# Raw expert weights loaded through the Activation queue during the attention stage of an attention + mixture-of-experts + MLP kernel

## The chip, the cores and the metric

The kernel runs on one core of a Trainium2 chip. The metric is the device time of one execution in microseconds. Before the change it is 692.5 us, the median of 3 runs (692.36 to 692.69).

## What is computed

Three layers follow each other. The first is causal attention with a decay (the running sum of log f) on 2 batches, 8 heads, 576 positions, 64 values a head. The second is a dense mixture of 4 experts with ReLU, weighted by normalised domain probabilities, and the third an MLP with x * sigmoid(1.702 x).

```python
def _attn_ref(q, k, v, f):
    scores = scale * np.matmul(q, k.transpose(0, 1, 3, 2))
    cum = np.cumsum(np.log(np.clip(f, 0.0001, 1.0)), axis=-1)
    scores = np.where(causal, -1e9, scores + cum[..., :, None] - cum[..., None, :])
    attn = softmax(scores)
    return np.matmul(attn, v)

def _moe_ref(x, domain_probs, w1, w2):           # x: 1152 x 512, E = 4, F = 1024
    p = domain_probs / (domain_probs.sum(-1, keepdims=True) + 1e-09)
    for e in range(E):
        out += p[:, e:e + 1] * (np.maximum(x @ w1[e], 0.0) @ w2[e])

def _moe2_ref(x, w_in, w_out):                   # F = 2048
    h = x @ w_in
    return (h * (1.0 / (1.0 + np.exp(-1.702 * h)))) @ w_out
```

## The kernel before

Products are made of rounded parts: each operand is split into a high part (rounded to float32r) and a low part (what is left), and three products of the parts are summed. A weight tile of 128 x 512 is split in two steps, by `split_w` (line 213): ScalarE (ACT) writes the high part `whi` (`round_act`, line 60), and later `rest` lets VectorE (DVE) write the low part `wlo` (line 230). Raw weights come two tiles at a time into a buffer `wst` of 512 KB (`load_owed`, line 188), of which there are four. A buffer is free once DVE has made the low parts of both its tiles.

The program runs over steps. The list `seq` holds units of work of the mixture (layer 1 or 2 of a visit of an expert half to a chunk of tokens), each unit a few steps. In the first 200 us the same loop also pulls the attention forward (`pull`), a pair of heads at a time: scores on TensorE (PE, line 587), the row maximum on DVE (617), the exponential on ACT (633), the normalisation by GpSimd (POOL, 643), transposes on PE (661), copies `ph` by ACT (line 60), the product with v on PE (691), and the split of its result into `xh` and `xl`. PE works on layer 1 (line 866) and layer 2 (1016) of the experts in between. Everything after `begin_late` (the joint products, line 904, and the MLP) has no attention in it.

The loads of the heads (`kq`, `qr`, `cb`, `cbs`, `vd`: keys, queries, the running sums spread over partitions, values) and those of the raw weights are all issued by SyncE (SP) through `load` (line 66), in one order. `cb` and `cbs` must wait until DVE has read the buffer that they overwrite, in its maximum of an earlier unit.

When a pair of weight tiles has been split, `rest` puts `load_pair` into `pair_due`, and it is called by the `rest` of the next tile that is split:

```python
        def rest():
            while pair_due:
                pair_due.pop()()
            (nc.gpsimd if v_ == 0 and kind == 'a' and g < 4 else nc.vector).tensor_sub(lf, raw, f(hf))
            if g % 2:
                ...
                pair_due.append(load_pair)
```

The order of each engine's instructions isn't the order of the code: the framework sets it by a scheduler that follows its own estimate of times, except where the code pins it (`in_turn`, `pin_turn`).

Of the kernel before, what the change touches and what calls it, by code (L numbers as in the profile page):

```python
# [39 lines left out]
def attn_moe_mlp(ctx: ExitStack, tc: tile.TileContext, qk0, qk1, qk2, v0, vp, fg, dp, wa_moe, wb_moe, wa_mlp, wb_mlp, out):  # L40
# [6 lines left out]
    nc = tc.nc  # L47
# [16 lines left out]
    def load(out, in_):  # L64

        ins = nc.sync.dma_start(out=out, in_=in_)
        if start[0]:
            tc.keep_in_program_order(ins)
# [8 lines left out]
    late = {}  # L77
# [16 lines left out]
    def scratch(i, o):  # L94
        return h_raw[i][:, o:o + 4 * WN]

    def tiles(c):

        t0, n = span[c]
        return range(t0 // 128, (t0 + (2 * n if c == EXP[0] else n)) // 128)  # L100
# [90 lines left out]
    def load_owed():  # L191

        while w_owed[0] and w_loaded[0] < len(w_pairs):
            kind, v_, g = w_pairs[w_loaded[0]]
            b = visits[v_][0]
            if b < NMOE:
                src = (wa_moe if kind == "a" else wb_moe)[b, g:g + 2]
            else:
                i = m_order.index((kind, v_, g))
                if m_made[0] < i + 2:  # L200
                    return
                src = wm[i:i + 2]
            w_owed[0] -= 1
            w_loaded[0] += 1
            t = wst_p.tile([128, 2, 512], F32, tag="wst", name="wst")
            load(t, src.rearrange("g p c -> p g c"))
            raw_w[kind, v_, g] = t[:, 0, :]
            raw_w[kind, v_, g + 1] = t[:, 1, :]

    lo_due, pair_due, lo_of = [], [], []  # L210

    def split_w(kind, v_, g):
        while (kind, v_, g) not in raw_w:
            next(cv_gen[0])
            load_owed()
        raw = raw_w.pop((kind, v_, g))
        p = wa_p if kind == "a" else late["wb"] if late and v_ % 2 else wb_p
        hi = p.tile([128, 4, 128], F32R, tag="hi", name="whi")
        lo = p.tile([128, 4, 128], F32R, tag="lo", name="wlo")
        hf = hi.rearrange("p a c -> p (a c)")  # L220
        lf = lo.rearrange("p a c -> p (a c)")
        round_act(hf, raw)
        (wa if kind == "a" else wb)[v_, g] = (hi, lo)
        if kind == "a" and v_ in joint:
            joint_raw[g] = raw
# [6 lines that stand above are left out]
                if kind == "a" and v_ in joint and v_ not in placed:  # L232
                    sum_weights(v_, g // 2)
                pair_due.append(load_pair)

        lo_due.append(rest)
        lo_of.append((kind, v_, g))
# [87 lines left out]
    def split_rest():  # L325
        lo_of.clear()
        while lo_due:
            lo_due.pop(0)()
# [82 lines left out]
    def begin_late():  # L411
        att_scope.close()
        start[0] = False
        late["ps"] = pool("ps_l", 5, PSUM)
        late["st"] = pool("mst", 2)
        late["wf"] = pool("wf", 2)
        late["h2"] = pool("h2", 1)
        late["ts"] = pool("ts", 1)
        late["ws"] = pool("ws", 1)
        late["jr"] = pool("jr", 2)  # L420
        late["tr"] = pool("tr", 1)
        late["jc"] = pool("jc", 2)
        late["t"] = pool("cv", 2)
        late["cd"] = pool("cd", 1)
        late["wb"] = pool("wb2", 4)
        late["rs"] = pool("rs", 1)
        hbuf[0] = tuple(late["h2"].tile([128, 4, WN], F32R, name=n) for n in ("hh2", "hl2"))
        acc.append(late["rs"].tile([128, 4, 512], F32, name="acc1"))
        for _ in range(2):
            mlp_load()  # L430
# [631 lines left out]
    t = scratch(0, 0)  # L1062
    fr, cum = t[:16, :S], t[:16, S:2 * S]
    t = scratch(1, 0)
# [65 lines left out]
    def drain(c):  # L1130
        while ready[0] < c:
            pull()
# [50 lines left out]
    def split_until(kind, v_, gs):  # L1183
        while any((kind, v_, g) in split_q for g in gs):
            split_next()
        if any((kind, v_, g) in lo_of for g in gs):
            split_rest()
# [40 lines left out]
    for i, (kind, v_, b, c) in enumerate(seq):  # L1228
        if kind == 1 and c < NCH:
            drain(c)  # L1230
        if not late and ready[0] == NCH - 1 and i >= need[-1][0]:
            begin_late()
            cv_gen[0] = mlp_convert()
            ts_gen = sum_tokens(EXP)
        u, m = (kind, v_, b, c), visits[v_][1].index(c)
        if u == (1, v_mlp, NMOE, MLP[0]):
            ts_gen = sum_tokens(MLP)
        nxt = [(j, cc) for j, cc in need if j > i]
        if kind == 3:
            for _ in ts_gen:  # L1240
                pass
            split_until("a", v_, range(4))
            split_rest()
            while (v_, m) not in ws:
                split_sums()
            j_gen = emit_joint(v_, b, m)
        n_steps = steps(kind, v_, b, c)
        for g in range(n_steps):
            if kind in (2, 6):
                split_until("b", v_, range(4))  # L1250
            elif kind not in (4, 5):
                split_until("a", v_, [g] if kind == 1 else range(4))
            if i == 0:
                ev = lambda: None
            elif kind == 3:
                ev = next(j_gen)
            else:
                if kind in (4, 5) and ("b", v_, 2 if kind == 5 or g > 4 else 0) in lo_of:
                    split_rest()
                ev = (emit_l1(v_, b, c, g) if kind == 1 else emit_l2(v_, b, c, g) if kind == 2 else  # L1260
                      emit_l2(v_, b, c, g + len(tiles(c)) - OVER) if kind == 6 else emit_l2_joint(v_, b, c, g, kind == 5))
            for _ in range(sums_at.get(u, 0)):
                in_turn(next, ts_gen, None)
            if sum_due and kind != 6:
                split_sums_done()
            if kind == 3 and g == 6:
                j_done.add((v_, m))
            n = 0
            if nxt:
                j, cc = nxt[0]  # L1270
                left = sum(steps(*u) for u in seq[i:j]) - g
                n = max(0, -(-(due[cc] - pulled[0]) // left))
                for _ in range(n):
                    pull()
            rests = []
            for d in split_due[:]:
                d[0] -= 1
                if d[0] == 0:
                    split_due.remove(d)
                    rests.append(split_output(d[1]))  # L1280
            if g == 0:
                for what, args in place_at.get((u, -1), ()):
                    what(*args)
            low_now = lows[:]
            lows.clear()
            evac[0]()
            for l_, q, h_ in low_now:
                nc.vector.tensor_sub(l_, q, f(h_))
            for r in rests:
                r()  # L1290
            evac[0] = ev
            split_next()
            if len(split_q) > 4:
                split_next()
            for what, args in place_at.get((u, g), ()):
                what(*args)
            if v_ + 1 < len(visits) and not v_exp <= v_ < v_all:
                if u == last_l1[v_] and kind == 1:
                    split_q.append(("a", v_ + 1, g))
                elif u == last_l1[v_] and g in (3, 5):  # L1300
                    split_q.append(("a", v_ + 1, g // 4))
                if u == last_l2[v_] and g == n_steps - 1 and v_ + 1 != v_exp:
                    split_q.extend(("b", v_ + 1, k) for k in range(4))
            if late:

                if sums_at.get(u, 0) < 2:
                    cv_due[0] += ((0.75 if kind == 4 else 0) if v_ < v_all else 1.4 if b < NMOE else 1.3) * (4 / n_steps)
                while cv_due[0] >= 1:
                    in_turn(next, cv_gen[0], None)
                    cv_due[0] -= 1  # L1310
                load_owed()
            if v_ >= v_exp:
                pinned = v_ < v_all or v_ == v_all and kind == 3
                (pin_engines.add if pinned else pin_engines.discard)(nc.tensor.engine)
                pin_turn()
            else:
                pin_from[1] = len(nc.cur_bb.bb.instructions)
# [58 lines left out]
```

## Time and profile before

| what | value |
|---|---|
| runs, median of 3 | 692.5 us (692.36 to 692.69) |
| the profiled execution | 693.89 us, its span 692.2 us |
| granted clock of TensorE | 0.999 of full speed |
| PE busy | 681.9 us, 99% of the span |
| DVE, ACT, POOL busy | 505.4, 341.7, 222.3 us |
| chain that ended last | PE 94%, DMA 2%, others 1% or less |

The profile covers one execution. Its span runs from the first to the last instruction; the 1.7 us between span and time lie around it. A share of busy time is a mean over stages that differ: the attention stage (to about 200 us) is the only one that the change touches, and it has to be read from that stage's windows and timelines. A busy PE counts matmuls that overlap in the array, so a short wait can hide in the tail of the matmul before it.

### The profile page before, as it was taken

What the parts mean: (1) busy time and instruction counts of PE and PEld (TensorE: products, weight loads), DVE (VectorE), ACT (ScalarE), POOL (GpSimd) and SP (SyncE); (2) the same over time, 40 slices, a digit from 0 to 9 for tenths busy, and PEclk for the clock granted to TensorE, in tenths of its full rate; (3) what the DMA queues carried; (4) which work ended last, traced back from release to release, by engine and by line L of the source; (5) the groups of instructions that cost most, each with busy time, mean ns of one, the idle gap of its engine ahead of it and who ended that gap; (6) DMA issues with size and microseconds to landing.
All of it is one profiled execution on the core that took longest, in us unless ns stands there. A gap on an engine that the chain in (4) does not pass through costs nothing.

```text
span 692.2 us, 10730 instructions
## 1 busy us (share of the span) xinstructions
PE 681.9 (99%) x3829; PEld 596.3 (86%) x3829; DVE 505.4 (73%) x1057; ACT 341.7 (49%) x789; POOL 222.3 (32%) x266
## 2 busy tenths in 40 slices
PE   8998999999999999999999999999999999999997
PEld 4787888888988998898888888888899998998986
DVE  6886677766569678686876788777699798786632
ACT  5768677666532735734334344343457462551420
POOL 6877576532133554515105114112004202200000
PEclk9999999999999999999999999999999999999999
DMA  7696636341312144142422452344132244221012
GB/s 258 224 303 236 232 122 242 92 118 73 104 48 65 58 122 147 52 137 78 140 103 82 148 152 78 121 152 143 56 107 76 77 157 158 81 93 45 1 46 91
DMA packets 38597, 83.37 MB, mean 120 GB/s; under 512 B 3560, under 2 KB 3568, under 8 KB 38544
## 3 DMA queue, kind: packets, MB, share of 16 engines
q1 hardware_dynamic: 38504, 82.65, 36.1%
q8 instruction: 30, 0.49, 0.3%
q14 instruction: 23, 0.19, 0.1%
q10 hardware_dynamic: 40, 0.04, 0.0%
HBM read 71.88 MB, written 10.78 MB: 119 GB/s over the span
## 4 chain that ended last, share of the span: by engine, by line
PE 94%; DMA 2%; POOL 1%; DVE 1%; ACT 1%; issue 0%; SPq 0%; POOLq 0%; ACTq 0%
PE m L1016 43%; PE m L866 20%; PE m L904 19%; PE s L587 4%; PE x L691 4%; PE t L661 3%; DMA wst<-in_wa_moe_dram 1%; PE m L1161 1%; DMA dpraw<-in_dp_dram 1%; POOL ks L513 0%; PE m L883 0%; POOL e L643 0%; PE t L735 0%; PE m L1077 0%; POOL qlo L531 0%
## 5 line engine op out<-in xcount | busy, mean ns | idle before, releaser
L1016 PE MATMUL m<-whi,hh 128*128 128x512 f32 x432 | 121.7, 392 | 0.0
L1016 PE MATMUL m<-whi,hl 128*128 128x512 f32 x432 | 119.6, 390 | 0.0
L1016 PE MATMUL m<-wlo,hh 128*128 128x512 f32 x432 | 119.2, 390 | 0.0
L230 DVE TENSOR_TENSOR wlo<-wst,whi 128x512 fp32r<-128x512 f32 x140 | 105.2, 767 | 7.6 <-ACT whi L60 7.1
L1016 PEld LDWEIGHTS m<-wlo,hh 128*128 128x128 f32 x432 | 80.9, 188 | 16.9
L1016 PEld LDWEIGHTS m<-whi,hl 128*128 128x128 f32 x432 | 80.9, 188 | 16.8
L60 ACT ACTIVATE whi<-wst 128x512 fp32r<-128x512 f32 x144 | 85.4, 625 | 17.3 <-DMA wst<-in_wa_moe_dram 7.4
L1016 PEld LDWEIGHTS m<-whi,hh 128*128 128x128 f32 x432 | 79.5, 188 | 13.9
L914 POOL TENSOR_TENSOR hl<-jc,hh 128x320 fp32r<-128x320 f32 x42 | 39.6, 945 | 156.5 <-ACT hh L60 151.6
L251 POOL TENSOR_TENSOR sr<-wst 128x256 f32<-128x256 f32 x20 | 18.1, 903 | 150.0 <-DVE tl L306 47.8
L866 PE MATMUL m<-xh,whi 128*128 128x256 f32 (+2 forms) x304 | 64.3, 327 | 0.3 <-DVE hl L1005 0.3
L866 PE MATMUL m<-xh,wlo 128*128 128x256 f32 (+2 forms) x304 | 64.3, 325 | 0.0
L866 PE MATMUL m<-xl,whi 128*128 128x256 f32 (+2 forms) x304 | 63.9, 326 | 0.0
L643 POOL TENSOR_SCALAR e<-e,sm 128x128 f32<-128x128 f32 (+4 forms) x72 | 45.5, 642 | 54.9 <-DVE sm L641 29.0
L912 ACT ACTIVATE jc<-jc 128x320 f32<-128x320 f32 x42 | 19.7, 469 | 75.3 <-DVE jc L910 75.3
L1049 DVE SCALAR_TENSOR_TENSOR acc<-m,dpn,acc 128x512 f32<-128x512 f32 x63 | 46.6, 744 | 11.0 <-PE m L1016 11.0
L866 PEld LDWEIGHTS m<-xh,whi 128*128 128x128 f32 x304 | 50.4, 189 | 3.8 <-DVE hl L1005 0.6
L866 PEld LDWEIGHTS m<-xh,wlo 128*128 128x128 f32 x304 | 50.6, 189 | 2.5
L866 PEld LDWEIGHTS m<-xl,whi 128*128 128x128 f32 x304 | 50.2, 189 | 2.6
L633 ACT ACTIVATE e<-e,mx 128x128 f32<-128x128 f32 (+4 forms) x72 | 41.6, 581 | 12.2 <-DVE mx L617 11.5
L999 ACT ACTIVATE m<-m 128x384 f32<-128x384 f32 x48 | 23.0, 479 | 35.6 <-DVE m L910 33.1
L931 ACT ACTIVATE u<-m 128x320 f32<-128x320 f32 (+1 forms) x20 | 9.0, 451 | 62.7 <-PE m L904 62.7
(141 smaller groups left out, 1326.3 us busy)
## 6 DMA issues: line engine op xcount, KB each, us to landing
wst<-in_wa_moe_dram SPq DMA_DIRECT2D x28, 512.0 KB, 3.7
wst<-in_wb_moe_dram SPq DMA_DIRECT2D x28, 512.0 KB, 4.2
mst<-in_wa_mlp_dram SPq DMA_DIRECT2D x16, 512.0 KB, 4.0
wm<-wf SPq DMA_DIRECT2D x32, 256.0 KB, 3.4
mst<-in_wb_mlp_dram SPq DMA_DIRECT2D x16, 512.0 KB, 3.8
wst<-wm SPq DMA_DIRECT2D x16, 512.0 KB, 3.6
cb<-cumd SPq DMA_DIRECT2D x16, 256.0 KB, 3.9
qr<-in_qk_dram SPq DMA_DIRECT2D x8, 384.0 KB, 5.2
```

The source lines that it names most:

```text
L60: return nc.scalar.activation(out=out, in_=in_, func=AF.Copy)
L230: (nc.gpsimd if v_ == 0 and kind == 'a' and g < 4 else nc.vector).tensor_sub(lf, raw, f(hf))
L587: nc.tensor.matmul(pt[:, :z - a], lhsT=lr[i][0], rhs=lr[i][1], start=i == 0 and not (both and pt is not bank), stop=i == n - 1, skip_group ...
L633: nc.scalar.activation(out=e[:, off:off + w], in_=e[:, off:off + w], func=AF.Exp, scale=-1.0, bias=mx, accum_out=sm[:, 0, k:k + 1])
L643: nc.gpsimd.tensor_scalar(out=e[:, off:off + w], in0=e[:, off:off + w], scalar1=sm[:, 0, i:i + 1], scalar2=1.0, op0=ALU.mult, op1=ALU.mult)
L691: nc.tensor.matmul(pt[64 * g:64 * g + 64, o:n], lhsT=lhsT, rhs=rhs, start=i == 0, stop=i == nk - 1)
L866: nc.tensor.matmul(p[:, :n], lhsT=w[:, k, :], rhs=x[c][:, k, :], start=(j == 0 and k == 0), stop=(j == 2 and k == 3))
L904: nc.tensor.matmul(p[:, :WN], lhsT=w[a][:, k, :], rhs=x[z][:, k, :], start=start and j == 0 and k == 0, stop=stop and j == 2 and k == 1, s ...
L914: nc.gpsimd.tensor_sub(hl[:, g, :], r, f(hh[:, g, :]))
L999: nc.scalar.activation(out=p[:, :n], in_=p[:, :n], func=AF.Gelu_apprx_sigmoid)
L1016: nc.tensor.matmul(p, lhsT=h_tile(v_, b, c, j, x, k), rhs=wb[v_, k][w].rearrange("p a c -> p (a c)"), start=i == 0 and k == 0, stop=i == 2 ...
L1049: nc.vector.scalar_tensor_tensor(out=a, in0=p, scalar=d, in1=a, op0=ALU.mult, op1=ALU.add)
```

## The change

While attention runs (not `late`) and once the loop over steps has begun (`units_begun` holds something), the pair load is issued by `nc.scalar`, ACT's own DMA queue, instead of SP's. And `pair_due` is emptied at the head of every step, so that the load stands in the step after the one in which the pair's last low part was put in, and doesn't wait for the `rest` of another tile.

```diff
@@ load_owed
             t = wst_p.tile([128, 2, 512], F32, tag="wst", name="wst")
-            load(t, src.rearrange("g p c -> p g c"))
+            if units_begun and not late:
+                nc.scalar.dma_start(out=t, in_=src.rearrange("g p c -> p g c"))
+            else:
+                load(t, src.rearrange("g p c -> p g c"))
@@
     lo_due, pair_due, lo_of = [], [], []
+    units_begun = []
@@ the loop over steps
         for g in range(n_steps):
+            units_begun.append(1)
+            if not late:
+                while pair_due:
+                    pair_due.pop()()
             if kind in (2, 6):
                 split_until("b", v_, range(4))
```

25 of the weight loads move from SP to ACT. On SP the rows of the heads' loads then follow each other without them; after the attention stage the order of all engines is as before. Names of tiles end in a number that counts what was built, so the same tile has another number after the change, and lines are 4 or 8 higher.

**ACT where the first loads stand.** Before, no load stands on ACT. `whi_1014` and `whi_1082` split the buffer that SP loads fourth.

```order
L633 ACTIVATE e_568,sm_569<-e_568,mx_572 128x384
L633 ACTIVATE e_600,sm_601<-e_600,mx_602 128x512
L633 ACTIVATE e_600,sm_601<-e_600,mx_604 128x512
L60 ACTIVATE whi_885<-wst_512 128x512
L60 ACTIVATE whi_945<-wst_512 128x512
L60 ACTIVATE ks_652<-kq_574 64x576 x2
L60 ACTIVATE whi_1014<-wst_646 128x512
L60 ACTIVATE whi_1082<-wst_646 128x512
L633 ACTIVATE e_639,sm_640<-e_639,mx_644 128x576
```

Of the change:

```order
L637 ACTIVATE e_570,sm_571<-e_570,mx_574 128x384
L637 ACTIVATE e_602,sm_603<-e_602,mx_604 128x512
L207 DMA wst_701<-in_wa_moe_dram 128x2x512
L637 ACTIVATE e_602,sm_603<-e_602,mx_606 128x512
L207 DMA wst_824<-in_wa_moe_dram 128x2x512
L60 ACTIVATE whi_887<-wst_512 128x512
L60 ACTIVATE whi_945<-wst_512 128x512
L60 ACTIVATE ks_652<-kq_576 64x576 x2
L60 ACTIVATE whi_1014<-wst_551 128x512
L60 ACTIVATE whi_1082<-wst_551 128x512
L637 ACTIVATE e_641,sm_642<-e_641,mx_646 128x576
L207 DMA wst_1017<-in_wa_moe_dram 128x2x512
```

The loads of `wst_701` (before `wst_753`) and `wst_824` (before `wst_942`) now stand between and behind the exponentials of a unit, ahead of the splits of `wst_512`.

**ACT where the next visit's weights are split.** Before:

```order
L60 ACTIVATE ph_609<-t_663 128x4x128
L1004 ACTIVATE hh_545<-m_824 128x256
L60 ACTIVATE whi_1086<-wst_753 128x512
L633 ACTIVATE e_687,sm_688<-e_687,mx_689 128x384
L1004 ACTIVATE hh_545<-m_888 128x256
L60 ACTIVATE whi_1146<-wst_753 128x512
```

Of the change:

```order
L60 ACTIVATE ph_611<-t_663 128x4x128
L1008 ACTIVATE hh_545<-m_826 128x256
L60 ACTIVATE whi_1086<-wst_701 128x512
L207 DMA wst_1089<-in_wa_moe_dram 128x2x512
L637 ACTIVATE e_687,sm_688<-e_687,mx_689 128x384
L1008 ACTIVATE hh_545<-m_890 128x256
L60 ACTIVATE whi_1146<-wst_701 128x512
```

The load of `wst_1089` stands behind `whi_1086` and ahead of the next exponential. It overwrites the buffer of `wst_551`, and so has to wait for DVE's `wlo` of `whi_1082`.

**PE and POOL about one pair of heads later.** PE before, from the scores of the unit behind to the transposes of `e_815` (the last 4 of the 12):

```order
L587 MATMUL s<-ks,qlo_0_132 128x384 x2
L866 MATMUL m<-xh,wlo 128x256 x4
L866 MATMUL m<-xl,whi 128x256 x4
L661 MATMUL t<-identr,e 128x128 x12
L866 MATMUL m<-xh,whi 128x256 x2
```

Of the change:

```order
L591 MATMUL s<-ks,qlo_0_132 128x384 x2
L870 MATMUL m<-xl,whi 128x256
L870 MATMUL m<-xh,whi 128x256 x4
L870 MATMUL m<-xh,wlo 128x256 x4
L870 MATMUL m<-xl,whi 128x256 x4
L870 MATMUL m<-xh,whi 128x256 x2
L665 MATMUL t<-identr,e 128x128 x8
L870 MATMUL m<-xh,whi 128x256
L591 MATMUL s<-ks,qhi 128x512
L594 MATMUL s<-tri,identr 128x128
L591 MATMUL s<-ks,qlo_0_132 128x512
```

POOL before:

```order
L643 TENSOR_SCALAR e<-e,sm 128x576
L57 TENSOR_SCALAR qhi<-qr 128x512
L531 TENSOR_TENSOR qlo_0_134<-qr,qhi 64x2x128 x2
L643 TENSOR_SCALAR e<-e,sm 128x384 x2
L611 MEMSET e 128x64
L643 TENSOR_SCALAR e<-e,sm 128x512 x2
```

Of the change:

```order
L647 TENSOR_SCALAR e<-e,sm 128x576
L647 TENSOR_SCALAR e<-e,sm 128x384 x2
L57 TENSOR_SCALAR qhi<-qr 128x512
L615 MEMSET e 128x64
L535 TENSOR_TENSOR qlo_0_134<-qr,qhi 64x2x128 x2
L647 TENSOR_SCALAR e<-e,sm 128x512 x2
```

PE now has 15 layer 1 products where it had 8 ahead of the first eight transposes, and more of them and of scores between those and the four of `e_815`. POOL normalises the unit of 384 before it splits the next queries, not after.

## Rows read from the trace of the kernel before

**Rows 1.** The page, part 1: busy time, share, instructions by engine.

```profile
PE 681.9 (99%) x3829; PEld 596.3 (86%) x3829; DVE 505.4 (73%) x1057; ACT 341.7 (49%) x789; POOL 222.3 (32%) x266
```

**Rows 2.** Windows: us, busy us of PE, PEld, DVE, ACT, POOL, clock, DMA, GB/s.

```profile
34.00:45.00 11.00, 11.00 (x68) 9.76 (x68) 10.94 (x27) 9.40 (x22) 8.99 (x10) 1.00 0.98 309
34.00:66.00 32.00, 29.70 (x209) 26.35 (x209) 26.03 (x70) 22.76 (x58) 24.76 (x28) 1.00 0.80 263
66.00:100.00 34.00, 34.00 (x236) 29.33 (x235) 22.66 (x73) 24.47 (x68) 21.55 (x27) 1.00 0.62 209
100.00:200.00 100.00, 100.00 (x698) 85.19 (x698) 63.73 (x188) 62.48 (x173) 40.27 (x54) 1.00 0.35 117
```

**Rows 3.** Timeline of PE, 45 to 64 us: start, us, line, operation, [idle before].

```profile
45.08 0.64 PE L866 MATMUL m<-xh,wlo 128*128 128x256 f32 x4
45.55 0.64 PE L866 MATMUL m<-xl,whi 128*128 128x256 f32 x4
...
46.63 0.60 PE L661 MATMUL t<-identr,e 128*128 128x128 f32 x4
46.99 0.61 PE L866 MATMUL m<-xh,wlo 128*128 128x256 f32 x3
...
50.70 0.71 PE L661 MATMUL t<-identr,e 128*128 128x128 f32 x5
51.73 0.75 PE L866 MATMUL m<-xh,whi 128*128 128x256 f32 x4 [0.32 <-DVE hl L1005]
52.31 0.40 PE L866 MATMUL m<-xh,wlo 128*128 128x256 f32 x2
53.24 0.40 PE L587 MATMUL s<-ks,qhi 128*128 128x288 f32 x1 [0.53 <-DVE mx L617]
...
60.58 1.04 PE L661 MATMUL t<-identr,e 128*128 128x128 f32 x8
63.06 0.66 PE L661 MATMUL t<-identr,e 128*128 128x128 f32 x4 [1.45 <-POOL e L643]
```

**Rows 4.** Timeline of ACT: an exponential, and the splits that waited for a weight load.

```profile
38.44 0.73 ACT L633 ACTIVATE e<-e,mx 128x512 f32<-128x512 f32 x1 [1.19 <-DVE mx L617]
...
45.10 0.39 ACT L1004 ACTIVATE hh<-m 128x256 fp32r<-128x256 f32 x1
49.72 0.63 ACT L60 ACTIVATE whi<-wst 128x512 fp32r<-128x512 f32 x1 [4.23 <-DMA wst<-in_wa_moe_dram]
...
62.66 1.15 ACT L60 ACTIVATE whi<-wst 128x512 fp32r<-128x512 f32 x2 [3.21 <-DMA wst<-in_wa_moe_dram]
...
85.24 1.15 ACT L60 ACTIVATE whi<-wst 128x512 fp32r<-128x512 f32 x2 [3.04 <-DMA wst<-in_wb_moe_dram]
```

**Rows 5.** Timelines of SP and DVE about the first of those loads.

```profile
41.44 1.09 SPq L66 DMA_DIRECT2D cbs<-cumd  x2
42.62 0.54 SPq L66 DMA_DIRECT2D wst<-in_wa_moe_dram  x1
...
35.14 2.58 DVE L230 TENSOR_TENSOR wlo<-wst,whi 128x512 fp32r<-128x512 f32 x2
```

**Rows 6.** Durations of a load's issue (min/median/max ns) and its landing; one that ACT issued.

```profile
L66 SPq DMA_DIRECT2D wst<-in_wa_moe_dram x28: 367/378/1171, 6.7 to 384.0; - x28
DMA to landing us min/median/max: 3.3/3.7/8.4
...
5.65 0.37 ACTq L1111 DMA_DIRECT2D cumd<-raw  x1
```

**Rows 7.** Timeline of DVE where the buffer of the fourth pair comes free.

```profile
44.44 3.04 DVE L230 TENSOR_TENSOR wlo<-wst,whi 128x512 fp32r<-128x512 f32 x2
```

**Rows 8.** Timeline of POOL ahead of the longest wait of PE.

```profile
51.76 1.17 POOL L57 TENSOR_SCALAR qhi<-qr 128x512 fp32r<-128x512 f32 x1 [1.50 <-DMA qr<-in_qk_dram]
54.64 1.16 POOL L643 TENSOR_SCALAR e<-e,sm 128x384 f32<-128x384 f32 x2
62.26 0.74 POOL L643 TENSOR_SCALAR e<-e,sm 128x576 f32<-128x576 f32 x1
```

## Prediction, made before the changed kernel ran

> **What bounds the kernel now.** I read four views, in this order. First the busy times of the page: PE is busy 681.9 of 692.2 us [rows 1], so at most 10.3 us of the span are PE idle, and only what shortens PE's own waits shortens the kernel. Second the windows, to find where that idle lies within the stage that the change touches: in 34 to 66 us PE is busy 29.70 of 32.00 us, in 66 to 100 it is busy 34.00 of 34.00 and in 100 to 200 all of 100.00 [rows 2]. The orders first differ at about 33 us, so there are 2.30 us of idle to be had, all of it before 66 us. Third PE's timeline in that stretch, for what each wait cost and who ended it [rows 3]. Fourth the timelines of ACT, SP, DVE and POOL around these waits, to see whether a weight load stands behind them.
>
> PE's timeline has three waits. The idle in brackets (0.32, 0.53 and 1.45 us, together 2.30) leaves out the time that hides in the tail of the matmul before, so I also price them by starts. Four layer 1 products take 0.47 us from start to start (45.08 to 45.55), or 0.118 each; four transposes 0.36 (46.63 to 46.99), or 0.09 each. Five transposes at 50.70 should let the next start at 51.15; it starts at 51.73: 0.58 lost. Two products at 52.31 should end in a start at 52.55; it is 53.24: 0.69 lost. Eight transposes at 60.58 should end in a start at 61.30; it is 63.06: 1.76 lost [rows 3]. Together 3.03 us by starts, 2.30 by idle.
>
> The first two waits come out of ACT. ACT stood 4.23 us in front of a split, until 49.72, because the weights were not there [rows 4]; then the eviction that frees PE's bank (`hh` by ACT, `hl` by DVE) and the maximum behind DVE's low part ran late, and they are what ended PE's waits at 51.73 and 53.24. Why the load was late is seen on SP: DVE had made the low parts that free the buffer by 37.72 (35.14 + 2.58), yet the load was issued at 42.62, behind `cbs` at 41.44, which waits for a maximum of DVE in another unit [rows 5]. So the load stood some 5 us in a queue for a reason not its own. The next load cost ACT another 3.21 us, until 62.66 [rows 4].
>
> The third wait is POOL's: it normalised the unit of 576 only at 62.26, after a stretch in which it ran without a pause from 51.76 on, and ahead of that it had stood 1.50 us for queries (`qr`) [rows 8].
>
> **The change, part by part.** The profiled execution took 693.89 us and its span 692.2; the sum is made as a difference against that execution, and carried over to the median of 692.5, which is 1.39 us below it. About 0.2% (1.4 us) is what a measurement of this kernel can tell from no change.
>
> *Earlier loads.* The first ACT load that matters now stands behind an exponential that had ended by 37.25 us (38.44 - 1.19) [rows 4], so it goes some 5 us earlier; with the landing of 3.3 to 8.4 us [rows 6] it is there between 41 and 46, where ACT comes to its split at 45.5 (45.10 + 0.39) [rows 4]. The next one goes behind the exponential of 38.44, at about 39.2 [rows 4]. So both waits of ACT, 4.23 + 3.21 = 7.44 us, go but for at most half a microsecond. With the first, PE's 0.58 + 0.69 = 1.27 us go (0.85 by idle).
>
> *The third wait.* POOL now normalises the unit of 384 (1.16 us) ahead of the query split, in the time in which it stood 1.50 us, so its chain to the unit of 576 comes about 1.2 us earlier; and PE has seven more layer 1 products ahead of the first eight transposes and three of them with a whole score group behind, about 10 x 0.118 = 1.2 us, before it needs that unit. Together 2.4 against 1.76, less the 1.27 by which PE itself comes earlier: 1.1 of the 1.76 surely, the rest if nothing else is late. By idle it is 1.45.
>
> *The issues on ACT.* 25 loads go to ACT. The trace shows no weight load there; the nearest rows are SP's for the same transfer, 0.378 us in the middle and 1.171 at most, and ACT's own for a small transfer, 0.37 [rows 6]. I take 0.38, which both agree on, and keep 1.17 for the slow end. In 34 to 66 us ACT is busy 22.76 us and idle 9.24 [rows 2], of which 7.44 is the wait for weights; 1.80 is other waiting. By the order, eight loads fall in this stretch (8 x 0.38 = 3.0 us) and three more splits of 0.62 us come forward into it (1.9). That gives 22.76 + 3.0 + 1.9 + 1.80 = 29.5 us of ACT for a stretch that would last 32.0 - 2.3 = 29.7. It just fits, and it is why I take the 2.30 us by idle and not the 3.03 by starts. From 66 us ACT has 9.53 us idle in 34 and 37.5 in 100 [rows 2], and 17 issues are 6.5 us: hidden. That cover is real: ACT stood 3.04 us for weights until 85.24 [rows 4] in a stretch where PE lost nothing.
>
> *SP without the weights.* 25 issues of 0.38 us leave SP. That lets `vd`, `kq` and `qr` go a little earlier; no PE wait hangs on it but through the 1.50 us of POOL, counted above. After 200 us every engine's order is the old one and the stage moves as a whole. The emptied `pair_due` adds no instruction.
>
> Sum: -2.3 us, so 691.6 for an execution like the profiled one and **690.2 us** for the median. Bounds: a gain of 3.5 (all by starts, and half a microsecond of shorter PE order) and none.
>
> **The rivals.**
>
> *ACT gives it back (no change).* The loads land early, but issues and waits for DVE take ACT's place. For it: the account of ACT leaves only 0.2 us, and ACT's order can't use all idle. Against: the freed 7.44 us are more than the 4.9 put in. A gain of 0 to 1 is left: about 692.0 us. Chance 0.18.
>
> *The heads' loads pay (little change).* From 34 to 45 us the DMA engines are busy 98% of the time at 309 GB/s [rows 2]. There the load of 42.62 took until ACT's split at 49.72 [rows 4, 5], far over the 3.7 us in the middle [rows 6]. Two more pairs of 512 KB come forward into that stretch; at 309 GB/s they are 3.4 us of transfer. If all of it fell on `qr`, POOL's wait of 1.50 [rows 8] would grow by 3.4, of which the unit of 384 now covers 1.2; the unit of 576 would be 2.2 late, and the third wait stay or grow while the first two go: 691.8 us. Against: the queries also leave SP earlier. Chance 0.13. A rule of the Trainium skill says that outright (DMA: Bandwidth & Descriptors, section Issuing engines are not separate DMA queues): loads started by ScalarE and SyncE end up on the same 16 DMA engines and interleave, so a second queue gives no bandwidth. By that rule the change's gain would be only the order of issue, and this rival holds where the engines are full; the 98% agree with the condition, while no row here has weights on ACT's queue to show the interleaving.
>
> *ACT is blocked by its own loads (slower).* A load on ACT that waits for DVE holds everything behind it, exponentials, `ph` copies, evictions. The place is the load of `wst_1089`, put behind a split that would end at about 46.1 us (45.49 + 0.62): it needs DVE's second low part of a pair that ran from 44.44 to 47.48 [rows 7]. That is 1.4 us, with the first 384 exponential queued behind it. If every second load waits so, a load holds ACT 0.38 + 0.7 = 1.08 us, and ACT needs 22.76 + 1.9 + 1.80 + 8 x 1.08 = 35.1 us for the stretch: 3.1 more than the 32.0 it has, and about 695.6 us. It decides from 0.69 us a load on, where the sum is 32.0. For it: DVE is busy 26.03 of 32 there [rows 2], its low parts last up to 1.5 us each [rows 7]. Against: the load stands at most places well behind its low part, and where DVE is late, the maximum that the next exponential needs is late too, so that the wait costs nothing by itself. Chance 0.13.
>
> That the change doesn't do what it says is excluded by the order: the 25 rows are on ACT.
>
> **How the numbers follow.** The forecast has 0.54, with its own range 689.3 to 691.1. The three rivals have 0.18, 0.13 and 0.13; 0.02 is left for what I don't see. Faster by over 0.2% means below 691.1: nearly all of the forecast's chance (0.50) and a part of the second rival's (0.03), 0.53. Within 0.2% lie the first rival, most of the second and a rest of the others: 0.34. Slower is the third rival's: 0.13. The range goes from 689.0, near the gain of 3.5, to 693.6, which takes in both rivals around no change and leaves out most of the slower one.
>
> **What would show it.** In the profile after: no weight wait of ACT above 1 us in 34 to 66 us; PE busy to within 0.5 us in the same stretch; 25 `wst` issues on ACT's queue, with a middle near 0.38 us; the rest of PE's timeline the same, only earlier by 2 to 3 us. The sum is wrong if ACT's waits for weights go and PE's waits don't (then they were never ACT's), if an ACT row shows a wait for `wlo` in front of a load and an exponential late behind it, or if PE has new idle after 66 us, where now it has none.

## The result and the profile after

The changed kernel takes 696.19 us (median of 5 runs, 695.36 to 697.35), the kernel before in the same comparison 692.69 (692.36 to 693.63). The ratio is 1.0051, 95% interval 1.0037 to 1.0066: slower by 3.5 us, where 2.3 us of gain were forecast. The profiled execution after took 697.35 us, its span 695.6, which is 3.4 more than the span before. Two executions at a granted clock of 0.56 and 0.75, one of 1133.96 us of a kernel below and one of 841.08 of the kernel before, are left out of what follows.

First the question where the time lies. The windows of the changed kernel, with the columns of [rows 2]:

```profile
34.00:45.00 11.00, 9.72 (x56) 8.58 (x56) 8.22 (x23) 8.73 (x20) 8.16 (x11) 1.00 0.92 282
34.00:66.00 32.00, 28.41 (x201) 25.55 (x202) 25.88 (x66) 23.35 (x58) 22.26 (x25) 1.00 0.92 287
66.00:100.00 34.00, 32.53 (x227) 27.57 (x226) 23.27 (x65) 22.70 (x61) 20.55 (x24) 1.00 0.57 186
100.00:200.00 100.00, 100.00 (x702) 85.10 (x701) 65.02 (x198) 65.63 (x183) 43.48 (x61) 1.00 0.38 117
```

PE idle has moved, not gone. 34 to 45 us, full before [rows 2], now has 1.28 us of it, and 66 to 100 another 1.47; from 100 us on nothing is lost. PE's timeline of the changed kernel names the waits:

```profile
33.18 0.44 PE L591 MATMUL s<-ks,qlo 128*128 128x512 f32 x1
35.28 0.73 PE L1020 MATMUL m<-whi,hh 128*128 128x512 f32 x2 [1.67 <-ACT hh L896]
50.37 0.50 PE L591 MATMUL s<-ks,qhi 128*128 128x512 f32 x1 [0.74 <-DVE sm L644]
54.78 0.74 PE L870 MATMUL m<-xh,whi 128*128 128x256 f32 x4 [1.56 <-DVE hl L1009]
59.68 2.27 PE L695 MATMUL x<-ph,vd 128*64 128x320 f32 x20
68.99 0.66 PE L665 MATMUL t<-identr,e 128*128 128x128 f32 x4 [1.47 <-POOL e L647]
```

By idle these are 1.67 + 0.74 + 1.56 + 1.47 = 5.44 us against the 2.30 of [rows 3]: 3.1 of the 3.4 us that the span has grown. The row without a bracket at 59.68, the products with v of one pair of heads, is used as a milestone below.

ACT's timeline shows what stands behind the first and the third wait (ACTq is ACT's queue; a row of it starts when the load is issued, not when ACT began to wait for it), and DVE's the low parts that the fifth load waits for:

```profile
31.81 0.63 ACT L60 ACTIVATE whi<-wst 128x512 fp32r<-128x512 f32 x1 [1.57 <-PE m L887]
32.25 2.34 ACTq L207 DMA_DIRECT2D wst<-in_wb_moe_dram  x1
34.63 0.60 ACT L896 ACTIVATE hh<-m 128x512 fp32r<-128x512 f32 x1 [2.19 <-DVE mx L621]
...
41.46 1.15 ACT L60 ACTIVATE whi<-wst 128x512 fp32r<-128x512 f32 x2 [1.59 <-PE m L1020]
...
47.23 0.65 ACT L60 ACTIVATE whi<-wst 128x512 fp32r<-128x512 f32 x1
52.87 0.37 ACTq L207 DMA_DIRECT2D wst<-in_wa_moe_dram  x1
53.29 0.61 ACT L637 ACTIVATE e<-e,mx 128x384 f32<-128x384 f32 x1 [5.42 <-DMA cb<-cumd]
...
60.53 1.39 ACT L60 ACTIVATE ks<-kq 64x576 fp32r<-64x576 f32 x2 [0.89 <-DVE mx L621]
```
```profile
47.02 2.82 DVE L234 TENSOR_TENSOR wlo<-wst,whi 128x512 fp32r<-128x512 f32 x2
```

The weight waits of [rows 4] are gone, and two other stops have come, both at a load. At 32.25 the issue itself takes 2.34 us, and the eviction behind it comes at 34.63; the name in its bracket, a maximum that had ended a microsecond before, is the wrong one. This is the load of `wst_551`, the first of the 25; the orders ahead of the prediction begin with the second. The other stop is at the fifth load, of `wst_1089`, the one that the prediction's third rival named. ACT was done with the split at 47.88, and the load was issued at 52.87, with the exponential behind it. DVE's low parts, for which it has to wait, ended at 49.84 (47.02 + 2.82), so they are only 1.96 us of the 4.99. What ended the rest is told by the chain of waits (start, us, what) and by the landing times of the two loads of `cb`:

```profile
44.81 7.98 DMA cb<-cumd
52.87 0.37 ACTq L207
53.29 0.27 ACT e L637
```
```profile
cb<-cumd SPq DMA_DIRECT2D x2, 256.0 KB, 7.7
```

`cb` belongs to the heads and has nothing to do with `wst_1089`. They meet in a semaphore, a counter by which a load tells that it has landed: in the built program eight of these are handed in turn to all loads of both queues, and a load waits until the load eight places before it, which had the same one, has landed. The loads of the program in that order (number, semaphore, queue, tile):

```
38 6 SP cb_716
39 7 SP cb_717
40 0 ACT wst_824
41 1 SP cbs_720
42 2 ACT wst_1017
43 3 SP cbs_720
44 4 SP vd_848
45 5 SP kq_880
46 6 SP qr_882
47 7 ACT wst_1089
```

So the load of `wst_1089` waits for `cb_717`, and the queries `qr_882` wait for `cb_716`. SP's timeline agrees: `cb` goes at 44.31, and `qr` only at 51.77, where it went at 45.13 before (last row, of the kernel before).

```profile
44.31 0.89 SPq L66 DMA_DIRECT2D cb<-cumd  x2
...
51.77 0.80 SPq L66 DMA_DIRECT2D qr<-in_qk_dram  x2
```
```profile
45.13 4.64 SPq L66 DMA_DIRECT2D qr<-in_qk_dram  x2
```

From about 221 us on the two kernels run alike. The first joint product (first and last start in the middle of each row) marks the end of what differs, before and after:

```profile
L904 PE MATMUL m<-th,sh x48: 305/309/309, 218.2 to 309.9; 128*128 128x320 f32 x48
```
```profile
L908 PE MATMUL m<-th,sh x48: 305/309/309, 221.7 to 313.3; 128*128 128x320 f32 x48
```

It starts 3.5 us later, and what follows takes 474 us in both. In the experiments this start tells what the attention stage has cost in the profiled execution.

### The profile page after: what moved, and what is told of

Its sections match the earlier page's. It is cut to its first block, busy times and chain, and to the rows that moved or that the text cites. A ratio compares the mean times of both kernels' runs of the same rounds, so it can differ in the third digit from the quotient of the medians.

```text
span 695.6 us, 10704 instructions
## 1 busy us (share of the span) xinstructions
PE 683.5 (98%) x3828; PEld 596.7 (86%) x3829; DVE 508.0 (73%) x1057; ACT 342.6 (49%) x789; POOL 221.7 (32%) x266
## 4 chain that ended last, share of the span: by engine, by line
PE 91%; DMA 3%; POOL 2%; ACT 2%; DVE 1%; issue 1%; ACTq 0%; SPq 0%; POOLq 0%
PE m L1020 42%; PE m L870 20%; PE m L908 19%; PE x L695 3%; PE s L591 3%; PE t L665 3%; DMA cb<-cumd 1%; DMA wst<-in_wa_moe_dram 1%; ACT e L637 1%; PE m L1165 1%; DMA dpraw<-in_dp_dram 1%; POOL qlo L535 1%; POOL e L647 1%; ACT whi L60 0%; ACTq L207 0%
## 5 line engine op out<-in xcount | busy, mean ns | idle before, releaser
L1008 ACT ACTIVATE hh<-m 128x384 fp32r<-128x384 f32 (+1 forms) x68 | 26.3, 386 | 28.3 <-DVE hl L1009 19.5
```

What stands on the lines that cost most here:

```text
L1008: nc.scalar.activation(out=h_, in_=q, func=AF.Relu)
```

## The experiments

The first theory was: two stops of ScalarE at its own loads make the loss, the first by a slow issue, the second by a semaphore that the load shares with SyncE's slow load. Against it stood two rivals: full DMA engines, with ScalarE only showing it, and the earlier place of the load in the code. Every kernel was run beside the kernel before; the ratios have 95% intervals and need not equal the quotient of the medians.

| kernel | median, us | ratio to before (95%) | first joint product, us |
|---|---|---|---|
| before | 692.69 to 693.03 | 1 | 218.2 |
| the change | 696.19 | 1.0051 (1.0037 to 1.0066) | 221.7 |
| queue only | 696.11 | 1.0034 (1.0021 to 1.0046) | 220.7 |
| head of the step only | 693.44 | 1.0004 (0.9994 to 1.0014) | 217.8 |
| semaphore shifted | 697.48 | 1.0058 (1.0043 to 1.0072) | 221.1 |
| first load on SyncE | 696.19 | 1.0048 (1.0029 to 1.0066) | 220.5 |
| first and fifth on SyncE | 696.02 | 1.0050 (1.0038 to 1.0062) | 222.0 |
| 8 KB as first load | 696.89 | 1.0051 (1.0038 to 1.0064) | 221.1 |
| half the bytes | 696.43 | 1.0045 (1.0027 to 1.0062) | 218.9 |
| GpSimd's queue | 693.53 | 1.0007 (0.9994 to 1.0021) | 215.8 |
| the same again | 693.90 | 1.0013 (0.9998 to 1.0028) | 221.2 |
| GpSimd, first 8 | 692.56 | 0.9988 (0.9976 to 1.0001) | 217.3 |
| GpSimd, first 4 | 694.40 | 1.0022 (1.0009 to 1.0036) | 220.4 |
| GpSimd, queue only | 692.45 | 0.9989 (0.9981 to 0.9998) | 216.8 |

**Which half of the change.** One half alone, each way:

```diff
@@ queue only: the loop over steps
-            if not late:
-                while pair_due:
-                    pair_due.pop()()
@@ head of the step only: load_owed
-            if units_begun and not late:
+            if units_begun and not late and False:
```

> Loads on ScalarE's queue, but pair_due is emptied by the next split as before the change, not at the head of a step. Theory: both stops of ScalarE stand at the same places with the same waits, so 696.2 (695.6 to 696.8). Rival (the earlier place does the damage, the queue does not): 692.7.

> pair_due is emptied at the head of a step, but all loads stay on SyncE. Theory: ScalarE has no load in its way, PE's waits of 1.67 and 1.56 us are not there; the loads stand a step earlier behind the heads' loads, so that at most the 4.23 and 3.21 us of ScalarE's waits for weights shrink: 692.7 or down to 691.0. Rival (the earlier place does the damage): 695 to 696.5.

The queue alone is as slow as the whole change (696.11 for 696.19 us, with intervals that overlap), with the same stops of ACT (2.27 us of issue at 32.67, and 4.46 us ahead of the exponential at 52.34). The head of the step alone is the kernel before, within the interval. The rival of the earlier place falls, and the reason is in the order: on ACT the first load stands between the same two instructions, a split and the eviction of `hh`, whether the code issues it early or late.

The head of the step also shows what the prediction had hoped for. PE's first two waits are gone; a third of 1.34 us is left. The milestone, the products with v, comes at 55.71, where the change has it at 59.68 with the same work ahead of it by the order. PE is idle 0.8 us less in 34 to 66 us than before, and half of that is lost again by the joint products.

```profile
34.00:66.00 32.00, 30.52 (x219) 27.35 (x218) 27.20 (x70) 23.54 (x59) 24.92 (x27) 1.00 0.83 274
```

**The shared semaphore.** One more small load moves all later loads by one semaphore:

```diff
+    tiny = const.tile([128, 16], F32, name="tiny")
@@ load_owed, behind the load on nc.scalar
+                if w_loaded[0] == 10:
+                    load(tiny, wb_moe[0, 0][:, 0:16])
```

> The change with one more load, 8 KB on SyncE, put in so that the load of wst_1089 shares its completion semaphore with the weight load wst_825 instead of with cb; nothing is taken away. Theory: ScalarE's stop before the exponential falls from 5.42 us to about 2.4 (until VectorE's low part, which ended at 49.84), PE's 1.56 us at 54.78 shrinks by 1.0 to 1.5, the stop of 2.34 us stays: 696.2 - 1.2 = 695.0 (694.5 to 695.4). Rival (transfers, or the low part itself): nothing becomes free earlier, 696.2 or a little more.

The stop shrank as the theory said, and the load is now issued when DVE's low parts end (45.55 + 3.24 = 48.79). ACT's timeline:

```profile
48.82 0.41 ACTq L208 DMA_DIRECT2D wst<-in_wa_moe_dram  x1
49.29 0.62 ACT L640 ACTIVATE e<-e,mx 128x384 f32<-128x384 f32 x1 [1.92 <-DVE mx L624]
```

A load of 8 KB that nobody reads takes 3.5 us off ACT's stop. PE's waits at 50 and 54 us are gone, and its milestone comes at 56.56, 3.1 us earlier than in the change. So the semaphore is shown. But the joint products start only 0.6 us earlier and the median did not fall; POOL's and PE's timelines and the windows show where the 3.1 us went:

```profile
56.35 0.62 POOL L57 TENSOR_SCALAR qhi<-qr 128x512 fp32r<-128x512 f32 x1 [1.97 <-DMA qr<-in_qk_dram]
```
```profile
66.94 1.11 PE L668 MATMUL t<-identr,e 128*128 128x128 f32 x4 [2.53 <-POOL e L650]
```
```profile
66.00:67.00 1.00, 0.06 (x1) 0.07 (x2) 0.00 (x0) 0.00 (x0) 0.90 (x3) 0.91 1.03 398
67.00:68.00 1.00, 1.00 (x6) 1.00 (x6) 0.00 (x0) 0.00 (x0) 1.00 (x2) 0.50 0.72 147
69.00:70.00 1.00, 1.00 (x7) 1.00 (x7) 0.58 (x3) 0.98 (x3) 0.00 (x0) 0.50 0.50 197
```

POOL stood 1.97 us for queries that SP issues late for the same reason (`qr` waits for the semaphore of `cb`), the unit of 576 came late, and PE waited 2.53 us. Behind that wait the granted clock stood at 0.50, 1.2 in place of 2.4 GHz, from 67 to 70 us: some 1.5 us of work lost (half of 3). Most of the gain was given back at the third wait and behind it.

**The first load.** In one kernel it goes back to SP, in another the first and the fifth, in a third ACT keeps 8 KB of it:

```diff
@@ load_owed; second kernel: not in (8, 12)
-            if units_begun and not late:
+            if units_begun and not late and w_loaded[0] != 8:
@@ third kernel, in place of the load on nc.scalar
+                if w_loaded[0] == 8:
+                    nc.scalar.dma_start(out=t[:, 0, 0:16], in_=src[0][:, 0:16])
+                    load(t[:, 0, 16:512], src[0][:, 16:512])
+                    load(t[:, 1], src[1])
```

> Theory (two stops of ScalarE): the first moved load goes back to SyncE, the other 24 stay on ScalarE's queue. The stop of 2.34 us ahead of the eviction at 34.63 goes, and so PE's wait of 1.67 us at 35.28. The load of wst_1089 then shares its completion semaphore with an earlier weight load, not with cb, so ScalarE waits there for VectorE's low part alone: about 2.4 us in place of 5.42, and PE's 1.56 us at 54.78 shrinks to under 0.5. Time 696.2 - 1.5 - 1.1 to 1.6 = about 693.3 (692.7 to 693.9). If the 2.34 us is the price of whichever load stands first on ScalarE's queue, the issue of the next one (wst_701) takes over 1.5 us now. Rival (transfers): the loads are late because the DMA engines are full, ScalarE only shows it; then 24 of 25 loads on the same queue keep the time within 0.5 us of 696.2.

> The first and the fifth moved load go back to SyncE, 23 stay on ScalarE's queue; none of these stands at one of the two stops. Theory (two stops of ScalarE): both are gone, PE waits less than 0.5 us in 34 to 50; what is left is GpSimd's wait for queries and the unit of 576: 693 to 694.5. Rival (any load on ScalarE costs): 695.5 to 696.5 as first_sp.

> As first_sp, but of the first moved load ScalarE still brings 8 KB at the same place (16 columns of 1024) and SyncE the rest in two loads. If the 2.3 us belong to the place (something ScalarE's queue has to wait for at 32 us), the small load's issue takes over 2 us too and PE's wait of 1.6 us at 35 is there again; if they belong to the 512 KB transfer, it takes 0.4 us and there is no wait. Time: place 696.5 to 697.5, transfer 695.7 to 696.5.

The first two forecasts of the theory missed. With the first load on SP the slow issue and PE's wait of 1.67 are gone, the next load takes 0.44 us at 35.90, and the milestone comes at 57.0; but ACT has new stops at other loads (its timeline):

```profile
40.84 0.38 ACTq L207 DMA_DIRECT2D wst<-in_wa_moe_dram  x1
41.32 1.16 ACT L60 ACTIVATE whi<-wst 128x512 fp32r<-128x512 f32 x2 [2.50 <-DMA cbs<-cumd]
...
49.99 0.38 ACTq L207 DMA_DIRECT2D wst<-in_wa_moe_dram  x1
50.42 0.62 ACT L637 ACTIVATE e<-e,mx 128x384 f32<-128x384 f32 x1 [2.42 <-DVE mx L621]
```

Shared semaphores take part in both, with new partners. The third load (`wst_824`) now shares with `cb_581`, one of two loads that SP issued from 33.1 on and that landed 6.5 and 7.2 us later; DVE's low part had ended at 39.17. The fifth shares with the third, which took 9.1 us and landed at 49.92; DVE's low parts had ended at 49.27, so here the semaphore makes only the last 0.7 us. ACT stands 2.50 and 2.42 us there, and PE waits 0.62, 1.23 and 1.14. Without the fifth the stop at the third is still 2.54, and the fifth, issued by SP only at 66.08, leaves ACT 6.47 us without weights, with 2.18 us of PE wait. So it isn't two places: in both kernels another load of ACT's stream had a partner that was late, or was itself late on SP, so taking one out moved the stop. The theory is amended to that.

The 8 KB load shows that the slow issue is not a matter of size. ACT's and PE's rows, and a window behind:

```profile
32.17 2.76 ACTq L208 DMA_DIRECT2D wst<-in_wb_moe_dram  x1
35.03 1.09 ACT L901 ACTIVATE hh<-m 128x512 fp32r<-128x512 f32 x2 [2.66 <-DVE mx L626]
```
```profile
35.68 0.74 PE L1025 MATMUL m<-whi,hh 128*128 128x512 f32 x2 [2.15 <-ACT hh L901]
```
```profile
38.00:39.00 1.00, 1.00 (x4) 0.71 (x4) 1.00 (x3) 1.00 (x4) 0.00 (x0) 0.50 0.57 195
```

Five kernels have a load at this place, and all five take 2.2 to 2.8 us for its issue; a first load at 35.90 takes 0.44, so it isn't the queue's first use either. In all five, SP issues `qr`, both `cb` and the first `cbs` without a pause at that time, and ACT's issue ends some 0.1 us behind the last of these; but at 44.20 in the change a run of SP's loads as close left ACT's issue at 0.40 us, so that alone doesn't make it. What ACT's queue waits for there stays open. Its price is plain: 1.6 to 2.2 us of PE, and after 2.15 us again the clock of 0.50.

**Half the bytes.** This tells the rival of the full engines apart; every second weight tile of the moved loads is left out:

```diff
@@ load_owed
-                nc.scalar.dma_start(out=t, in_=src.rearrange("g p c -> p g c"))
+                nc.scalar.dma_start(out=t[:, 0:1], in_=src[0:1].rearrange("g p c -> p g c"))
...
-            raw_w[kind, v_, g + 1] = t[:, 1, :]
+            raw_w[kind, v_, g + 1] = t[:, 0 if units_begun and not late else 1, :]
```

> The change, but each of the 25 moved loads brings only the first tile of its pair (256 KB for 512), and both splits read that one; order, waits and shared semaphores are the same. Theory (semaphores are shared with SyncE's slow loads, which are slow because the DMA engines are full): cb lands in about 5 us for 7.7, so that ScalarE's stop ahead of the exponential falls from 5.42 to 2 to 3 us and the queries come 2 to 3 us earlier; the stop of 2.3 us at 32 us stays if it is not the size that makes it. 693.5 to 695. Rival (the orders of the engines alone do it, the bytes don't matter): 696.2 within 0.5.

`cb` lands in 5.7 us for 7.7 (the middle of its two loads), and `qr` goes at 46.85 for 51.77. ACT's stop at the fifth load ends with DVE's low part again, POOL waits 0.58 us for queries, and PE's waits at 50 and 54 us are gone:

```profile
48.92 0.33 ACTq L207 DMA_DIRECT2D wst<-in_wa_moe_dram  x1
49.40 0.62 ACT L637 ACTIVATE e<-e,mx 128x384 f32<-128x384 f32 x1 [1.91 <-DVE mx L621]
```

The slow issue (2.32 us) stays. The profiled execution took 694.52 us; three others of the five compared took 696.4 to 698.2 at a mean granted clock of 0.997 or 0.998, so the median, 696.43, does not show the gain and misses the forecast. What is shown is that the slow landings are part of the cause: a shared semaphore costs as much as the load that holds it is slow.

**Another queue.** The same loads on GpSimd's queue, which in the built program has semaphores of its own, with three variants:

```diff
@@ GpSimd's queue; first 8: and w_loaded[0] < 16; first 4: and w_loaded[0] < 12
-                nc.scalar.dma_start(out=t, in_=src.rearrange("g p c -> p g c"))
+                nc.gpsimd.dma_start(out=t, in_=src.rearrange("g p c -> p g c"))
@@ queue only: as above, and also
-            if not late:
-                while pair_due:
-                    pair_due.pop()()
```

> The 25 loads on GpSimd's queue in place of ScalarE's. They then share no completion semaphore with SyncE's loads. ScalarE has no stop of either kind; what GpSimd pays for an issue isn't known from a trace here. Theory: ScalarE's waits of 2.3 and 5.4 us are gone, but each load of GpSimd that waits for VectorE's low part holds the query splits and normalisations behind it, so PE's wait for the unit of 576 grows over 1.5 us: 692.5 to 696. Rival (weights that come early are enough): under 692.

> The kernel with all 25 loads on GpSimd's queue once more, for its spread and another trace. If the slow executions come from waits of PE that grow out of GpSimd's issues, a slower trace shows PE waiting for a normalised unit or for scores; if from the clock, a granted clock under 1 after a wait.

The two profiled executions of the same kernel, 691.53 and 696.99 us, differ in one wait. The window of the first and POOL's and PE's rows of the second:

```profile
34.00:66.00 32.00, 31.99 (x229) 29.03 (x228) 29.50 (x78) 26.92 (x67) 30.37 (x35) 1.00 0.96 321
```
```profile
58.74 0.62 POOL L57 TENSOR_SCALAR qhi<-qr 128x512 fp32r<-128x512 f32 x1 [4.68 <-DMA qr<-in_qk_dram]
```
```profile
66.72 0.66 PE L665 MATMUL t<-identr,e 128*128 128x128 f32 x4 [3.59 <-POOL e L647]
```

In the first, PE has no wait at all in 34 to 66 us, and the first joint product starts 2.4 us earlier than before: in this execution the 2.3 us of the prediction were there to be had, with the weights early and ACT not stopped. In the second POOL stood 4.68 us for `qr` (0.26 in the first), PE 3.59 behind it, and the granted clock was 0.50 from 68 to 71 us. SP issued these queries at 44.64 in the first and at 46.42 in the second, and they landed 9.3 and 12.2 us later. The DMA engines are busy 96% of 34 to 66 us in the first and 92% in the second. When the weights are taken early, what is late is the heads' queries, and by how much differs between executions: 12 of them lie between 691.5 and 695.9 us, 12 more between 691.6 and 697.1.

> Only the first eight of the 25 loads, those up to 66 us, on GpSimd's queue; the other 17 stay on SyncE, at the head of a step. Theory (ScalarE must not be stopped; what is to be had lies before 66 us): PE is busy all of 34 to 66 us as with all 25 on GpSimd, 2.3 us less than before: 690.5 to 691.5, and with fewer of GpSimd's issues behind 66 us a narrower spread than its 691.5 to 695.9. Rival (GpSimd's issues delay the unit of 576 in some executions already before 66 us): the spread stays, median 693.5.

> Only the first four loads on GpSimd's queue, the other 21 on SyncE. Theory: the first two waits of PE (0.32 and 0.53 us idle) go, GpSimd has 3 us less to issue before the unit of 576; but the fifth load stands on SyncE behind the heads' loads again, so ScalarE waits for weights at about 63 us and the third wait (1.45 us) stays in part: 691 to 692.5. Rival (GpSimd's issues themselves are what varies): spread of 4 us as with 25.

> All 25 loads on GpSimd's queue, pair_due emptied by the next split as before the change. Theory (the place in the code plays no part, the scheduler puts the load where its buffer comes free): the same as with the emptying, 691.5 to 695.9, median about 693.5. Rival (the emptying makes the loads wait on GpSimd): under 692 with a narrow spread.

With eight loads on GpSimd the median is 692.56, not clear of before, and the spread stays (691.1 to 696.3). With four it is slower; `qr` comes late again (1.38 us) and the third wait is 2.17 us. Both forecasts missed. The queue only is the steadiest kernel: 692.45 us, its 11 runs within 692.2 to 692.5, 0.11% under before with an interval that just leaves out 1. Its first load stands at 35.86 us, 2.9 later than with the emptying, the queries land 8.6 us after their issue, POOL never waits for them, and PE's only wait in 34 to 66 us is 0.60 at 48.83:

```profile
34.00:66.00 32.00, 31.39 (x225) 28.37 (x224) 30.10 (x74) 25.77 (x65) 29.32 (x35) 1.00 0.94 308
```

So here the place in the code does play a part, against the expectation. All 25 issues are on GpSimd and the spread is gone, so it isn't GpSimd's issues that vary. That later weights leave the DMA engines to the queries fits these three traces (8.6 us for 9.3 and 12.2), but no run shows it by itself.

## Why the prediction was wrong

*What bounds the kernel, and what there is to have.* Right. PE binds, 2.30 us of idle lie in 34 to 66 us, and one execution without the waits gained that much (31.99 us busy, the stage 2.4 us shorter).

*Earlier loads.* Right: ACT no longer waits for weights, and in the kernel with the head of the step alone the first two waits of PE go.

*The issues on ACT.* This step failed. "I take 0.38, which both agree on, and keep 1.17 for the slow end" is a price of the issue, and as such it holds:

```profile
L207 ACTq DMA_DIRECT2D wst<-in_wb_moe_dram x13: 374/374/2339, 32.2 to 192.6; - x13
```

Only the 2.34 at 32.25 lies far outside. But a load in an engine's stream also costs what it waits for, and that the account of 29.5 us put at nothing. Of the first eight loads (32.25 to 66.90 us) three hold ACT, for 2.19 + 5.42 + 0.89 = 8.5 us, or 1.06 a load, where the account had 0.38 and fitted by 0.2. (The 1.59 at 41.46 isn't theirs: the products of PE that this split needs end only at 41.32.) The Trainium skill states the same of the rows (Perfetto Trace Analysis, section DMA Instruction — HWDGE): the profiled part of a load begins when all its semaphores are satisfied, so its wait for them is outside it. The row at 52.87 agrees, with 0.37 us behind 4.99 us of standing.

*The third rival.* It had the place (`wst_1089`, behind `whi_1086`), the price (1.08 us a load, deciding from 0.69), and the time, 695.6 us against the measured 696.19. It was given 0.13, because "where DVE is late, the maximum that the next exponential needs is late too, so that the wait costs nothing by itself". That holds for the 1.96 us that the load waits for DVE. It doesn't hold for the other 3.0, which the prediction had not seen: the completion of an unrelated load on the other queue. The order of the program with its semaphores, which gives each load's partner, was there to read. The slow issue at 32 us was not seen by any rival. That the time came out so near is therefore in part luck: the rival had DVE's waits at every second load, and the runs showed one semaphore, one slow issue and little of DVE.

*The third wait of PE.* Wrong. It was to shrink by 1.1 of 1.76 us, since POOL normalises the unit of 384 ahead of the query split. But with ACT stopped, POOL stood 3.70 us for that unit's exponential with the split behind it, and the wait stayed at 1.47. POOL's timeline:

```profile
56.51 1.16 POOL L647 TENSOR_SCALAR e<-e,sm 128x384 f32<-128x384 f32 x2 [3.70 <-DVE sm L645]
57.63 1.07 POOL L57 TENSOR_SCALAR qhi<-qr 128x512 fp32r<-128x512 f32 x1
```

*The heads' loads.* The second rival, at 0.13, is not what made the change slow, for POOL doesn't wait for queries there; it shows once ACT is stopped less. With the semaphore shifted POOL waits 1.97 us for `qr`, issued late behind `cb`, and 4.68 in the slower trace on GpSimd's queue, where `qr` took 12.2 us to land. The rival's 691.8 us was too low for that: that execution took 696.99. The rule of the Trainium skill that was set beside it (DMA: Bandwidth & Descriptors, section Issuing engines are not separate DMA queues: loads of ScalarE and SyncE share the same 16 engines) agrees. With weights on ACT's queue the engines were 92% busy at 287 GB/s in 34 to 66 us, and SP's `cb` of 256 KB took 7.7 us to land, 5.7 with half of the weights' bytes. It had taken up to 7.8 before too (in 30 to 70 us), where no load of a computing engine stood behind it.

*SP without the weights, and the stage behind 66 us.* The loads left SP as forecast, but the queries went 6.6 us later (51.77 for 45.13), not earlier. From 100 us on PE loses nothing, as forecast.

The step that failed is thus the term for the issues on ACT: 8 x 0.38 = 3.0 us were put in, and ACT stood 8.5 us at these loads. The range ended at 693.6 and left out most of the slower case. With ACT's account fitting by only 0.2 us, that case should have had more than 0.13.

## What to carry to other kernels

A load that is moved into a computing engine's queue brings its waits along: before moving it, list for each load what it waits for, the buffer and the load that had its completion semaphore before, and compare that with when the engine comes to it. An engine whose stream has no slack behind the load shouldn't issue it, however short the issue; an engine with slack may do it without loss (here GpSimd, with semaphores of its own, at 692.45 us), though it gained almost nothing here. And where the DMA engines are nearly full, a transfer that goes earlier makes another later, so look at what the bounding engine waits for next.

## What the runs showed of the hardware that was not expected

- In five profiled executions PE had a wait of 2.15, 2.17, 2.18, 2.53 or 3.59 us, and each was followed by some 3 us at a granted clock of 0.50, which costs some 1.5 us beside the wait. In the nine others, the change with its waits of up to 1.67 us among them, the clock is not seen to fall in the attention stage.
- One place of ACT's queue took 2.2 to 2.8 us for an issue that takes 0.37 elsewhere, with 8 KB as with 512 KB; the cause is open.
- GpSimd's issue of a 512 KB load took 0.72 to 0.93 us in its timeline, twice the 0.37 to 0.38 usual on ACT; spans on GpSimd are rough.
